# phi_q@KV of two token tiles back to back, one sign per PSUM slot, and three more AB buffers in the space of the first layernorm

## The chip, the core and the metric

The kernel runs on one core of a Trainium2 chip. A core has five engines that run side by side and are ordered only by semaphores: TensorE (PE in the profile; its weight loads are PEld), VectorE (DVE), ScalarE (ACT), GpSimd (POOL) and SyncE (SP), whose queue issues the DMAs here. Matmuls write to PSUM, eight banks of 512 fp32 columns on 128 partitions; the other engines copy results from there to SBUF. The metric is the device time of one execution in microseconds (us): the median of the runs.

## The reference

One block of a transformer on x of 2048 tokens by 640 columns: layernorm, linear attention with 32 heads of 20 columns and a Hedgehog feature map, output projection, residual; then layernorm, a gated GELU feed-forward of width 1536, residual.

```python
pq = einsum("bhsd,hdf->bhsf", q, w_phi);  pk = einsum("bhsd,hdf->bhsf", k, w_phi)
phi_q = concatenate([softmax(pq), softmax(-pq)], -1)     # 20 + 20 features a head
phi_k = concatenate([softmax(pk), softmax(-pk)], -1)
kv  = einsum("bhsf,bhsd->bhfd", phi_k, v);  z = einsum("bhsf->bhf", phi_k)
num = einsum("bhqf,bhfd->bhqd", phi_q, kv)
den = einsum("bhqf,bhf->bhq", phi_q, z)[..., None] + 1e-6
h   = x + (num / den).reshape(B, S, D) @ wo
h2  = h + (gelu(ln(h) @ w_gate) * (ln(h) @ w_up)) @ w_down
```

## The kernel before

The tokens are 16 tiles of 128, in four blocks of four (b = t // 4). Everything is written in the order in which it is to be issued, engine by engine; semaphores come from a tile framework that tracks who writes and who reads each buffer.

*First part, to about 90 us.* Layernorm of x, transposed into LN1T (one tile of 5 x 512 bf16 columns a block), then v, k, their features, and the sums over tokens (kv). The q features are computed with the tokens along the free dimension: `q_mm` multiplies the folded weights Wq2 with LN1T into `pq`, and `q_exp` writes exp(pq) and exp(-pq) into the 13 tiles Eq. The last `pq` matmuls are the last readers of LN1T.

*Attention of a tile, in stages.* `attn_a_mm` (L500) computes `ab`: for each sign s (the two softmaxes) and each of 5 groups of heads, two matmuls of 64 rows by 88 columns, one for each half u of the partitions, which lie next to each other in TensorE's 128 rows. The 20 matmuls of a tile write two PSUM slots: half u of the heads in slot u, the sign in the slot's bank. `attn_a_ev` (L515) copies both to the SBUF tile AB of fp32, of which there are two. `attn_b` (L526), `attn_b2` and `attn_b3` turn AB into the normalised attention output `o`: products and sums on POOL (`pr`, `den`, `w`), the reciprocal `rd` and the big product `tt` on VectorE. A DMA transpose (`attn_t`) gives oT; `attn_c` multiplies with Wo into `po`; `attn_d` (L574) adds the residual on VectorE; `attn_d2` finds the second layernorm's statistics on ACT and POOL; `attn_e` normalises on ACT and transposes by DMA into LN2T.

*Feed-forward.* `gate_up(b, f, a0, a1)` (L610) computes one of 12 chunks of 128 hidden columns: ten matmuls into one slot `gu`, gate in bank 0 and up in bank 1; GELU on ACT; the product GT on VectorE. `down(b, tl, u)` (L623) computes one tile's output in two halves of 320 columns, u = 0 and 1, in the two banks of one slot `pd`, 12 matmuls each; after u = 1 a single VectorE add of 640 columns takes both banks and the residual to y, which is stored three units later. Only the very last tile evicts its halves apart, and there the second half takes a slot of its own (L627).

*PSUM.* After the first part the pool `psG2` (L490) has four slots of two banks, shared by pq, ab, po, gu and pd. A slot is handed on when its last reader is done; the first matmul of its next user waits for that.

*The order around the change.* `weave` (L657) walks through a list of units (12 `gate_up`, then `down`s), and before unit i issues every attention stage whose index is at most i. Stages whose index lies past the end of a list are carried to the next. `attn_at(t, i, offs)` places tile t's stages at i plus an offset each. Tiles 0 to 2 get their `ab` before the first unit; tile 3 at unit 1, tiles 4, 5, 6 at units 6, 9, 13 of the first list and 7 at the start of the second; tiles 8 to 15 at units 0, 2, 5, 7 of blocks 1 and 2. So each `ab` block but the first three stands alone between units of the feed-forward. TensorE, VectorE, ACT, POOL and SP each run their own instructions in this order.

Of the kernel before, what the change touches and what calls it, by code (L numbers as in the profile page):

```python
# [8 lines left out]
BF16 = mybir.dt.bfloat16  # L9
F32 = mybir.dt.float32  # L10
ALU = mybir.AluOpType
# [6 lines left out]
def kernel(  # L18
# [12 lines left out]
    nc = tc.nc  # L31
    P = 128
    S = 2048
    D = 640
    H = 32
# [3 lines left out]
    NB = NT // 4  # L39
    NC = D // P  # L40
    NF = FF // P
# [17 lines left out]
    KC = Dh + 2  # L59


    UH = H // 2
# [3 lines left out]
    o_v = out.rearrange("b (p t) d -> p (b t) d", t=NT)  # L66
# [10 lines left out]
    x_sb = [const.tile([P, 4, D], BF16, name=f"x_sb{b}") for b in range(NB)]  # L77
# [14 lines left out]
    def eq(t, c, s):  # L92
        for E, g in zip(Eq, QG):
            if t // 4 * NC + c in g:
                return E[:, g.index(t // 4 * NC + c), s, t % 4 * P:(t % 4 + 1) * P]

    def small(pool, shape, name, bufs=3):
        return pool.tile(shape, F32, name=name, bufs=bufs)

    def gtile(name):  # L100
        return psG.tile([P, 2, 512], F32, name=name, tag="G")
# [40 lines left out]
    def transpose_to(dst, src, on_pe, on_dve=False):  # L142

        if on_pe:
            tp = psG.tile([P, 16, P], BF16, name="tp", tag="G")
            for c in range(NC):
                nc.tensor.transpose(tp[:, c, :], src[:, c * P:(c + 1) * P], ident)
            (nc.vector.tensor_copy if on_dve else nc.scalar.copy)(dst, tp[:, 0:NC, :])  # L148
        else:
            nc.sync.dma_start_transpose(dst, src)  # L150


    mid = ctx.enter_context(tc.tile_pool(name="mid", bufs=1, side="right"))
    LN1T = [mid.tile([P, NC, 512], BF16, name=f"LN1T{b}") for b in range(NB)]
    Wq2 = mid.tile([P, NC, D], BF16, name="Wq2")
    p1_cm = tc.tile_pool(name="p1", bufs=1, reuse_waits="tile")
    p1 = p1_cm.__enter__()
# [99 lines left out]
    def ln_ap(t, on_act=False, on_pe=False):  # L257
# [3 lines left out]
        else:  # L261
            transpose_to(LN1T[t // 4][:, :, t % 4 * P:(t % 4 + 1) * P], ln, False)

    def ln_tp(t, on_dve=False):
        transpose_to(LN1T[t // 4][:, :, t % 4 * P:(t % 4 + 1) * P], lnp[t], True, on_dve)

    def lnT(t, c):
        b, tl = divmod(t, 4)
        return LN1T[b][:, c, tl * P:(tl + 1) * P]

# [85 lines left out]
    def q_mm(j):  # L356

        pqs[j] = gtile("pq")
        for i, bc in enumerate(QG[j]):
            b, c = divmod(bc, NC)  # L360
            for kc in range(NC):
                nc.tensor.matmul(pqs[j][:, i, :], lhsT=Wq2[:, kc, c * P:(c + 1) * P], rhs=LN1T[b][:, kc, :],  # L362
                                 start=(kc == 0), stop=(kc == NC - 1))

    def q_exp(j, signs=(0, 1)):
        for s in signs:
            nc.scalar.activation(Eq[j][:, :, s, :], pqs[j][:, 0:len(QG[j])], ACTF.Exp, scale=(1.0, -1.0)[s])  # L367
# [23 lines left out]
    def tr_c(t):  # L391
        transpose_to(LN1T[0][:, :, t * P:(t + 1) * P], xc[t], True, t == 1)

# [100 lines left out]
    p2r = ctx.enter_context(tc.tile_pool(name="p2r", bufs=1, side="right", reuse_waits="tile"))  # L494
    Wd = p2r.tile([P, NF, D], BF16, name="Wd")
    nc.sync.dma_start(Wd, B_w_down.rearrange("(c p) n -> p c n", p=P))

    LN2T, st = {}, {}

    def attn_a_mm(t):  # L500

        b = t // 4
        if b not in LN2T:
            LN2T[b] = p2.tile([P, NC, 512], BF16, name="LN2T", bufs=2)
        AB = p2r.tile([P, 2, H, KC], F32, name="AB", bufs=2)
        ab = gtile("ab"), gtile("ab")
        for s in range(2):
            for c in range(NC):
                for u, r in enumerate(HALF):
                    nc.tensor.matmul(ab[u][:, s, 3 * c * KC:(3 * c + 4) * KC], lhsT=eq(t, c, s)[r],  # L510
                                     rhs=KV[r, c, s].rearrange("p h f -> p (h f)"),
                                     start=(c == 0), stop=(c == NC - 1), skip_group_check=True)
        st[t] = AB, ab

    def attn_a_ev(t, dve=0):  # L515
        AB, ab = st[t]
        for u in range(2):
            (nc.vector.tensor_copy if u >= 2 - dve else nc.scalar.copy)(  # L518
                AB[:, :, u * UH:(u + 1) * UH].rearrange("p s h f -> p s (h f)"), ab[u][:, :, 0:UH * KC])
        st[t] = AB  # L520

    def attn_a(t, dve=0):
        attn_a_mm(t)
        attn_a_ev(t, dve)

    def attn_b(t, on_pe=False):  # L526

        eng = nc.vector if on_pe else nc.gpsimd
        AB = st[t]
        pr = small(p2, [P, H, 2], "pr", 2)  # L530
        eng.tensor_tensor(pr, AB[:, 0, :, Dh:KC], AB[:, 1, :, 0:KC:KC - 1], ALU.mult)
        den = small(p2, [P, H], "den", 2)
# [71 lines left out]
    def attn_e(t, on_pe=False, on_dve=False):  # L604
        if not on_pe:
            attn_ln(t)
        ln = st[t]
        transpose_to(LN2T[t // 4][:, :, t % 4 * P:(t % 4 + 1) * P], ln, on_pe, on_dve)
# [14 lines left out]
    def down(b, tl, u):  # L623
        if u == 0:
            st["pd"] = gtile("pd"), p2.tile([P, D], BF16, name="y", bufs=4)
        pd, y = st["pd"]
        if u == 1 and b == NB - 1 and tl == 3:  # L627
            pd = gtile("pd")
        last = b == NB - 1 and tl == 3

        cuts = [(0, 192), (192, HD)] if last and u == 1 else [(0, HD)]
        for n0, n1 in cuts:
            if n0:
                pd = gtile("pd")
            for f in range(NF):
                nc.tensor.matmul(pd[:, u, n0:n1], lhsT=st[b, "g", f][:, tl * P:(tl + 1) * P],  # L636
                                 rhs=Wd[:, f, u * HD + n0:u * HD + n1], start=(f == 0), stop=(f == NF - 1))
            if u == 1 or last:
                a = u if last else 0
                r = lambda x: x.rearrange("p (u f) -> p u f", u=2)[:, a:u + 1, n0:n1]  # L640
                nc.vector.tensor_tensor(r(y), pd[:, a:u + 1, n0:n1], r(x_sb[b][:, tl, :]), ALU.add)  # L641
                f0, f1 = a * HD + n0, u * HD + n1
                stores.append((lag, o_v[:, 4 * b + tl, f0:f1], y[:, f0:f1]))
                if b == NB - 1 and tl >= 2:
                    store(lag)

    later, stores, lag = [], [], 3

    def store(n):

        stores[:] = [(i - n, *x) for i, *x in stores]
        while stores and stores[0][0] <= 0:
            _, dst, src = stores.pop(0)
            nc.sync.dma_start(dst, src)


    def weave(units, stages):  # L657

        stages = sorted(later + stages, key=lambda x: x[0])
        later.clear()  # L660
        for i, (fn, *args) in enumerate(units):
            while stages and stages[0][0] <= i:
                _, g, *a = stages.pop(0)
                g(*a)
            store(1)
            fn(*args)
        later.extend((i - len(units), g, *a) for i, g, *a in stages)

    def gus(b, a0, a1):
        return [(gate_up, b, f, a0, a1) for f in range(NF)]  # L670

    def downs(b, tls):
        return [(down, b, tl, u) for tl in tls for u in range(2)]


    q_mm(q)
    attn_a(0, 1)
    q_exp(q)
    q_mm(q + 1)
    attn_b(0, True)  # L680
    attn_b2(0, True)
    attn_b3(0, True)
    attn_a(1, 1)
    q_exp(q + 1)
    q_mm(q + 2)
    attn_t(0)
# [21 lines left out]
        q_exp(j)  # L708
    attn_ln(1, True)
    attn_e(1, True, True)  # L710
    attn_a(2, 2)
    assert q + 9 == len(Eq)

    def attn_at(t, i, offs):

        fns = (attn_a, attn_b, attn_b2, attn_b3, attn_c, attn_d, attn_d2, attn_e)
        return [(i + o, fn, t) for fn, o in zip(fns, offs) if o >= 0]

    SHORT = (0, 2, 3, 4, 9, 9, 10, 12)
    SHORT2 = (0, 2, 3, 4, 10, 10, 11, 13)  # L720
    LONG = (0, 1, 2, 3, 6, 6, 7, 8)


    weave(gus(0, 0, 256) + downs(0, (0, 1)),
          attn_at(2, 0, (-1, 0, 1, 2, 7, 7, 8, 10)) + attn_at(3, 1, SHORT) + attn_at(4, 6, SHORT2) + attn_at(5, 9, SHORT2) +
          attn_at(6, 13, SHORT2))
    weave(gus(0, 256, 512) + downs(0, (2, 3)), attn_at(7, 0, SHORT))
    for b in range(1, NB):
        stages = []
        if b + 1 < NB:  # L730
            for tl in range(4):
                stages += attn_at(4 * b + 4 + tl, (0, 2, 5, 7)[tl], LONG)
        weave(gus(b, 0, 512) + downs(b, range(4)), stages)
    man_cm.__exit__(None, None, None)


# [28 lines left out]
```

## Time and profile before

| | |
|---|---|
| Time, median of 3 runs | 280.23 us (279.33 to 280.53) |
| Span of the profiled execution | 277.2 us; its own time is not listed apart from the runs |
| Granted TensorE clock | 1.000 |
| Busy share: PE, DVE, ACT, POOL | 98%, 60%, 52%, 34% |
| TensorE, `gu` matmuls 512 columns wide, all | 89.5 us busy |
| TensorE, `pd` matmuls, all | 53.8 us busy |
| TensorE, `ab` matmuls x320 | 9.1 us busy, 204 ns each |
| ACT copies AB<-ab, 704 columns | 28, 748 ns each |
| VectorE copies AB<-ab, 704 columns | 4, 886 ns each |
| VectorE adds y<-pd, 640 columns | 15, 823 ns each |

The span runs from the first to the last instruction of one execution; the time is measured around the whole program and is longer. In the groups, a row is: line, engine, operation, output<-inputs, shapes, count | busy time in all, mean ns of one | idle time of the engine just before them and what ended it. Busy time of matmuls counts overlapping ones once: they are pipelined, so the distance from one start to the next is shorter than one's length. In the timeline a row is start, length, engine, line, operation; what stands in brackets is the engine's idle time before it and the instruction that ended that. The chain is the work that ended last, followed back through whatever released each piece.

### The profile page before, as it was taken

To read this page: it belongs to the slowest core of one execution; us is meant where nothing else is said; L and a number is where in the kernel's file an instruction comes from. 1 tells how busy PE (TensorE), PEld (TensorE's weight loads), DVE (VectorE), ACT (ScalarE), POOL (GpSimd) and SP (SyncE) were. 2 spreads that over 40 slices of the span, in tenths; PEclk is the share of its full clock that TensorE was granted. 3 is DMA by queue.
4 is the path that set the end of the run, shared out by engine and by line. 5 is a ranking of instruction groups with operands and counts; after the bars stand their busy time and mean duration, and the time that the engine had idled before them with its cause. 6 is when DMAs were issued, how large, how long until landed. Compare 5 with 4: busy or idle time off the path is not lost.

```text
span 277.2 us, 5817 instructions
## 1 busy us (share of the span) xinstructions
PE 271.6 (98%) x2337; PEld 172.1 (62%) x2337; DVE 167.3 (60%) x292; ACT 143.5 (52%) x239; POOL 94.7 (34%) x213
## 2 busy tenths in 40 slices
PE   7899999999999999999999999999999999999995
PEld 3677777764555887788754555675455567444574
DVE  6799999899496776675325757322666622233222
ACT  4879998778598755374524364413445440222200
POOL 4348997765202217365301353400226230000000
PEclk9999999999999999999999999999999999999999
DMA  7965732489730021324120213130022413000011
GB/s 204 192 232 112 99 74 47 44 256 393 255 102 0 4 47 36 85 49 77 30 65 2 47 27 63 32 88 33 14 36 25 73 25 95 26 0 0 0 50 47
DMA packets 42235, 21.37 MB, mean 77 GB/s; under 512 B 35040, under 2 KB 40416, under 8 KB 42208
## 3 DMA queue, kind: packets, MB, share of 16 engines
q1 hardware_dynamic: 42208, 21.01, 30.8%
q8 instruction: 18, 0.29, 0.5%
q14 instruction: 9, 0.07, 0.1%
HBM read 10.18 MB, written 2.62 MB: 46 GB/s over the span
## 4 chain that ended last, share of the span: by engine, by line
PE 87%; SPq 3%; DMA 3%; DVE 2%; ACT 2%; issue 1%
PE gu L615 38%; PE pd L636 19%; PE pq L362 8%; PE po L570 8%; PE pk L274 5%; PE pv L274 4%; PE ab L510 3%; PE kvp L340 2%; SPq L186 2%; DMA LN1T<-ln 2%; DVE stats L110 1%; DMA WkT<-in_A_wqkv_dram 1%; ACT E L307 1%; ACT ln L134 1%; PE wa L228 1%
## 5 line engine op out<-in xcount | busy, mean ns | idle before, releaser
L621 DVE TENSOR_TENSOR GT<-gu,g 128x512 bf16<-128x512 f32 (+1 forms) x60 | 34.4, 580 | 54.3 <-ACT g L618 54.1
L618 ACT ACTIVATE g<-gu 128x512 bf16<-128x512 f32 (+1 forms) x60 | 30.7, 512 | 69.3 <-PE gu L615 68.5
L615 PE MATMUL gu<-LN2T,Wg 128*128 128x512 bf16 (+1 forms) x300 | 61.9, 337 | 0.1
L615 PE MATMUL gu<-LN2T,Wu 128*128 128x512 bf16 (+1 forms) x300 | 61.8, 337 | 0.0
L636 PE MATMUL pd<-Wd,GT 128*128 128x320 bf16 (+2 forms) x396 | 53.8, 295 | 0.0
L636 PEld LDWEIGHTS <-GT 128*128 128x128 bf16 x396 | 37.9, 98 | 15.3 <-DVE GT L621 0.9
L615 PEld LDWEIGHTS <-Wu 128*128 128x128 bf16 x300 | 29.3, 98 | 22.6
L615 PEld LDWEIGHTS <-Wg 128*128 128x128 bf16 x300 | 28.3, 98 | 20.8
L274 PEld LDWEIGHTS <-LN1T 128*128 128x128 bf16 x290 | 27.9, 98 | 11.0 <-DMA LN1T<-ln 0.3
L322 POOL TENSOR_TENSOR vt<-vS,rs 128x672 bf16<-128x672 bf16 x22 | 29.1, 1344 | 9.1 <-DVE rs L318 7.4
L641 DVE TENSOR_TENSOR y<-pd,x_sb 128x640 bf16<-128x640 f32 (+3 forms) x18 | 13.5, 749 | 30.2 <-PE pd L636 30.2
L518 ACT COPY AB<-ab 128x704 f32<-128x704 f32 x28 | 19.6, 748 | 19.8 <-PE ab L510 19.6
L551 DVE TENSOR_TENSOR tt<-AB,w 128x1280 bf16<-128x1280 f32 x16 | 23.8, 1486 | 1.0 <-POOL w L544 0.9
L570 PE MATMUL po<-Wo,oT 128*128 128x320 bf16 x160 | 24.3, 299 | 0.0
L274 PE MATMUL pk<-Wk,LN1T 128*128 128x320 bf16 x160 | 24.0, 299 | 0.0
L314 DVE TENSOR_REDUCE sk<-E 128x64 f32<-128x1280 bf16 x16 | 22.9, 1434 | 1.2 <-ACT E L307 1.2
L362 PE MATMUL pq<-LN1T,Wq 128*128 128x512 bf16 x100 | 22.9, 379 | 0.0
L367 ACT ACTIVATE Eq<-pq 128x1024 bf16<-128x1024 f32 (+1 forms) x26 | 19.9, 830 | 2.4 <-PE pq L362 2.4
L307 ACT ACTIVATE E<-pk 128x640 bf16<-128x640 f32 x28 | 18.3, 716 | 4.5 <-PE pk L274 4.3
L570 PEld LDWEIGHTS <-oT 128*128 128x128 bf16 x160 | 15.6, 98 | 7.0 <-ACT oT L148 0.3
L274 PE MATMUL pv<-Wv,LN1T 128*128 128x320 bf16 x130 | 19.8, 299 | 0.2 <-DMA LN1T<-ln 0.2
L134 ACT ACTIVATE ln<-x_sb,v,rstd 128x640 bf16<-128x640 bf16 x14 | 12.9, 919 | 11.3 <-POOL v L598 11.1
(101 smaller groups left out, 268.1 us busy)
## 6 DMA issues: line engine op xcount, KB each, us to landing
out_dram<-y SPq DMA_DIRECT2D x15, 160.0 KB, 1.8
Wg<-in_B_w_gate_dram SPq DMA_DIRECT2D x1, 1920.0 KB, 9.4
Wu<-in_B_w_up_dram SPq DMA_DIRECT2D x1, 1920.0 KB, 15.3
Wd<-in_B_w_down_dram SPq DMA_DIRECT2D x1, 1920.0 KB, 7.9
x_sb<-in_A_x_dram SPq DMA_DIRECT2D x2, 640.0 KB, 5.5
Wo<-in_A_wo_dram SPq DMA_DIRECT2D x1, 800.0 KB, 11.1
x_sb<-in_A_x_dram SPq DMA_DIRECT2D x4, 160.0 KB, 3.1
Wv<-in_A_wqkv_dram SPq DMA_DIRECT2D x2, 320.0 KB, 4.1
```

The lines of the kernel that those rows point to most:

```text
L274: nc.tensor.matmul(ps[:, u, 0:HD], lhsT=lnT(t, c), rhs=W[:, c, u * HD:(u + 1) * HD], start=(c == 0), stop=(c == NC - 1))
L307: nc.scalar.activation(Ek[t][:, s, :].rearrange("p (u f) -> p u f", u=2), pk[:, :, 0:HD], ACTF.Exp, scale=((lnp[t][2], nrstd[t]) if t in C ...
L314: nc.vector.reduce_sum(sk, Ek[t].rearrange("p s (h f) -> p (s h) f", f=Dh), axis=AX.X)
L322: eng.tensor_tensor(vt[:, s], vS[t % 8], rs[:, s * H:(s + 1) * H, None].to_broadcast([P, H, VC]), ALU.mult)
L362: nc.tensor.matmul(pqs[j][:, i, :], lhsT=Wq2[:, kc, c * P:(c + 1) * P], rhs=LN1T[b][:, kc, :], start=(kc == 0), stop=(kc == NC - 1))
L367: nc.scalar.activation(Eq[j][:, :, s, :], pqs[j][:, 0:len(QG[j])], ACTF.Exp, scale=(1.0, -1.0)[s])
L551: nc.vector.tensor_tensor(tt.rearrange("p s (h f) -> p s h f", f=Dh), num, w[:, :, :, None].to_broadcast([P, 2, H, Dh]), ALU.mult)
L570: nc.tensor.matmul(po[:, u, 0:HD], lhsT=st[t][:, c, :], rhs=Wo[:, c, u * HD:(u + 1) * HD], start=(c == 0), stop=(c == NC - 1))
L615: nc.tensor.matmul(gu[:, i, 0:n], lhsT=W[:, c, f * P:(f + 1) * P], rhs=LN2T[b][:, c, a0:a1], start=(c == 0), stop=(c == NC - 1))
L618: nc.scalar.activation(g[:, 0:n], gu[:, 0, 0:n], ACTF.Gelu_apprx_tanh)
L621: nc.vector.tensor_tensor(st[b, "g", f][:, a0:a1], gu[:, 1, 0:n], g[:, 0:n], ALU.mult)
L636: nc.tensor.matmul(pd[:, u, n0:n1], lhsT=st[b, "g", f][:, tl * P:(tl + 1) * P], rhs=Wd[:, f, u * HD + n0:u * HD + n1], start=(f == 0), sto ...
```

## The change

Four edits go together.

1. *One sign per slot.* A slot of `ab` now holds both halves u of one sign s (`ab[s][:, u]`), so the first slot is complete after 10 of the 20 matmuls. `attn_a_ev` copies one sign, or one half of it, on the engine it is given.
2. *Pairs.* `attn_pair(t)` issues the 40 matmuls of tiles t and t + 1 in a row, in all four slots, and then five copies: the first slot half on ACT and half on VectorE, the second on ACT, the third on VectorE, the fourth on ACT. Tiles 2 to 15 go in seven pairs; 0 and 1 stay single, one slot on ACT and one on VectorE.
3. *Five AB buffers.* The four LN1T tiles become views of one fp32 tile, and three more AB buffers are views of the same memory.
4. *Places.* The pairs stand before unit 0 (tiles 2, 3), at units 7 and 14 of the first list, 14 and 16 of the second, and 18 and 20 of block 1; an index equal to the list's length means the start of the next list. All later stages keep the unit they had. In the five `down` tiles listed in AHEAD, the halves are 384 and 256 columns and each is added to y by itself; a pair follows right after each of these five tiles.

```diff
-    LN1T = [mid.tile([P, NC, 512], BF16, name=f"LN1T{b}") for b in range(NB)]
+    LN1F = mid.tile([P, NB * NC * 256], F32, name="LN1T")
+    LN1T = [LN1F.bitcast(BF16).rearrange("p (b c n) -> p b c n", b=NB, c=NC)[:, b] for b in range(NB)]
...
+    ABs = [p2r.tile([P, 2, H, KC], F32, name=f"AB{i}") for i in range(2)]
+    ABs += [LN1F[:, i * 2 * H * KC:(i + 1) * 2 * H * KC].rearrange("p (s h f) -> p s h f", s=2, h=H) for i in range(3)]
...
-        AB = p2r.tile([P, 2, H, KC], F32, name="AB", bufs=2)
+        AB = ABs[t % len(ABs)]
...
-                    nc.tensor.matmul(ab[u][:, s, 3 * c * KC:(3 * c + 4) * KC], lhsT=eq(t, c, s)[r],
+                    nc.tensor.matmul(ab[s][:, u, 3 * c * KC:(3 * c + 4) * KC], lhsT=eq(t, c, s)[r],
...
-    def attn_a_ev(t, dve=0):
+    def attn_a_ev(t, s, eng, us=(0, 2)):
         AB, ab = st[t]
...
+        eng(AB[:, s].rearrange("p (u h) f -> p u (h f)", u=2)[:, us[0]:us[1]], ab[s][:, us[0]:us[1], 0:UH * KC])
+
+    def attn_a(t):
         attn_a_mm(t)
-        attn_a_ev(t, dve)
+        attn_a_ev(t, 0, nc.scalar.copy)
+        attn_a_ev(t, 1, nc.vector.tensor_copy)
+        st[t] = st[t][0]
+
+    def attn_pair(t):
+        attn_a_mm(t)
+        attn_a_mm(t + 1)
+        attn_a_ev(t, 0, nc.scalar.copy, (0, 1))
+        attn_a_ev(t, 0, nc.vector.tensor_copy, (1, 2))
+        attn_a_ev(t, 1, nc.scalar.copy)
+        attn_a_ev(t + 1, 0, nc.vector.tensor_copy)
+        attn_a_ev(t + 1, 1, nc.scalar.copy)
+        for i in (t, t + 1):
+            st[i] = st[i][0]
...
+        if (b, tl) in AHEAD:
+            f0, f1 = ((0, 384), (384, D))[u]
+            for f in range(NF):
+                nc.tensor.matmul(pd[:, u, 0:f1 - f0], lhsT=st[b, "g", f][:, tl * P:(tl + 1) * P],
+                                 rhs=Wd[:, f, f0:f1], start=(f == 0), stop=(f == NF - 1))
+            nc.vector.tensor_tensor(y[:, f0:f1], pd[:, u, 0:f1 - f0], x_sb[b][:, tl, f0:f1], ALU.add)
+            if u == 1:
+                stores.append((lag, o_v[:, 4 * b + tl, :], y))
+            return
...
-    attn_a(2, 2)
+    attn_pair(2)
...
+    EARLY = (0, 1, 2, 7, 7, 8, 10)
+    SHORT = (0, 1, 2, 8, 8, 9, 11)
+    LONG = (0, 1, 2, 5, 5, 6, 7)
+    AHEAD = {(0, 0), (0, 2), (0, 3), (1, 2), (1, 3)}
...
+          attn_at(2, 0, EARLY) + attn_at(3, 3, EARLY) + [(7, attn_pair, 4)] + attn_at(4, 8, SHORT) + attn_at(5, 11, SHORT) +
+          [(14, attn_pair, 6)] + attn_at(6, 15, SHORT) + attn_at(7, 18, EARLY))
+    weave(gus(0, 256, 512) + downs(0, (2, 3)),
+          [(14, attn_pair, 8), (16, attn_pair, 10)] + attn_at(8, 17, LONG) + attn_at(9, 19, LONG) + attn_at(10, 22, LONG) +
+          attn_at(11, 24, LONG))
+    weave(gus(1, 0, 512) + downs(1, range(4)),
+          [(18, attn_pair, 12), (20, attn_pair, 14)] + attn_at(12, 21, LONG) + attn_at(13, 23, LONG) +
+          attn_at(14, 26, LONG) + attn_at(15, 28, LONG))
+    for b in (2, 3):
+        weave(gus(b, 0, 512) + downs(b, range(4)), [])
```

More of the change, by code (lines that the diff above doesn't have):

```diff
@@ L513, in attn_a_mm @@
         st[t] = AB, ab
-    def attn_a_ev(t, dve=0):
+    def attn_a_ev(t, s, eng, us=(0, 2)):
         AB, ab = st[t]
[L517 to L522, printed above, removed]
-        attn_a_mm(t)
-        attn_a_ev(t, dve)
+        eng(AB[:, s].rearrange("p (u h) f -> p u (h f)", u=2)[:, us[0]:us[1]], ab[s][:, us[0]:us[1], 0:UH * KC])
+    def attn_a(t):
+        attn_a_mm(t)
+        attn_a_ev(t, 0, nc.scalar.copy)
[11 more added lines that the diff above has]
+            st[i] = st[i][0]
     def attn_b(t, on_pe=False):
@@ L676 @@
     q_mm(q)
-    attn_a(0, 1)
+    attn_a(0)
     q_exp(q)
@@ L682 @@
     attn_b3(0, True)
-    attn_a(1, 1)
+    attn_a(1)
     q_exp(q + 1)
@@ L710 @@
     attn_e(1, True, True)
-    attn_a(2, 2)
+    attn_pair(2)
     assert q + 9 == len(Eq)
     def attn_at(t, i, offs):
[L716 to L721, printed above, removed]
-    weave(gus(0, 0, 256) + downs(0, (0, 1)),
[L725 to L733, printed above, removed]
+        return [(i + o, fn, t) for fn, o in zip((attn_b, attn_b2, attn_b3, attn_c, attn_d, attn_d2, attn_e), offs)]
+    EARLY = (0, 1, 2, 7, 7, 8, 10)
+    SHORT = (0, 1, 2, 8, 8, 9, 11)
+    LONG = (0, 1, 2, 5, 5, 6, 7)
+    AHEAD = {(0, 0), (0, 2), (0, 3), (1, 2), (1, 3)}
+    weave(gus(0, 0, 256) + downs(0, (0, 1)),
+          attn_at(2, 0, EARLY) + attn_at(3, 3, EARLY) + [(7, attn_pair, 4)] + attn_at(4, 8, SHORT) + attn_at(5, 11, SHORT) +
[8 more added lines that the diff above has]
+        weave(gus(b, 0, 512) + downs(b, range(4)), [])
     man_cm.__exit__(None, None, None)
```

## The prediction

> **What bounds the kernel now.** I read the engine shares and the clock on the page first, then the chain that ended last, then the timeline around one block of the edited matmuls, then the groups by form.
>
> ```profile
> PE 271.6 (98%) x2337; PEld 172.1 (62%) x2337; DVE 167.3 (60%) x292; ACT 143.5 (52%) x239; POOL 94.7 (34%) x213
> ...
> PEclk9999999999999999999999999999999999999999
> ...
> PE 87%; SPq 3%; DMA 3%; DVE 2%; ACT 2%; issue 1%
> ```
>
> TensorE is busy for the whole span at full clock, and the chain runs on it. From 92 us on that chain holds nothing but TensorE pieces, end to end, until the last eviction. So any time that TensorE loses or gains after 90 us is the kernel's time, and other engines count only where TensorE waits for them.
>
> Timeline around the `ab` block of tile 4 (start, length, engine, line):
>
> ```profile
> 97.48 0.71 PE L615 MATMUL gu<-LN2T,Wu 128*128 128x256 bf16 x5
> ...
> 98.12 0.57 PE L510 MATMUL ab<-KV,Eq 64*128 64x88 bf16 x20
> ...
> 98.62 0.72 PE L615 MATMUL gu<-LN2T,Wg 128*128 128x256 bf16 x5
> ```
>
> The 256-column matmuls start 0.109 us apart (ten take 1.09 in the chain), so the five from 97.48 are issued out at 98.03. The first `ab` starts 0.10 later. Its twenty go in ten pairs 0.039 apart (0.39 in all); then 0.11 is lost again before `gu` at 98.62. A block costs 0.60, of which 0.20 is getting in and out.
>
> Groups by form, timeline at the KV mask, at the second layernorm's first transposes, and on VectorE before the first `down`:
>
> ```profile
> L641 DVE TENSOR_TENSOR y<-pd,x_sb 128x640 bf16<-128x640 f32 x15 | 12.3, 823 | 28.6 <-PE pd L636 28.6
> ...
> L518 DVE COPY AB<-ab 128x704 f32<-128x704 f32 x4 | 3.5, 886 | 1.5 <-PE ab L510 1.5
> ...
> L641 DVE TENSOR_TENSOR y<-pd,x_sb 128x320 bf16<-128x320 f32 x1 | 0.5, 491 | 0.8 <-PE pd L636 0.8
> ```
> ```profile
> 71.20 0.51 ACT L349 COPY acc<-kvp 128x420 f32<-128x420 f32 x1 [0.82 <-DVE kvp L348]
> 71.74 0.59 DVE L352 TENSOR_TENSOR KV<-kvp,kmask 128x420 bf16<-128x420 f32 x1 [0.57 <-ACT acc L349]
> ```
> ```profile
> 90.34 0.49 DVE L148 COPY LN2T<-tp 128x640 bf16<-128x640 bf16 x1 [0.72 <-PE tp L147]
> ...
> 90.88 0.71 PE L615 MATMUL gu<-LN2T,Wg 128*128 128x256 bf16 x5
> 91.16 1.28 ACT L618 ACT_TABLE_LOAD   x1
> ```
> ```profile
> 111.41 0.35 DVE L540 RECIPROCAL rd<-den 128x32 f32<-128x32 f32 x1 [1.46 <-POOL den L533]
> ```
>
> The KV pair matters most: ACT reads one bank of the PSUM tile kvp, VectorE reads the other, they share no data, and VectorE still waited 0.57 for ACT. Waits here are kept per PSUM tile, not per bank. Handoffs: VectorE to TensorE 0.05 (90.83 to 90.88); TensorE to VectorE, TensorE to ACT and ACT to VectorE 0.03 to 0.04 (the last 128-column `pd` ended at 274.30 and its add began at 274.34).
>
> **The change, part by part.**
>
> *Joining blocks.* Seven pairs each drop one entry and one exit: 7 x 0.20 = -1.4 us. For pair 2 it is inside that pair's count below, so -1.2 for the other six. No offset in the stages behind an `ab` block moves: `attn_b` to `attn_e` of each tile keep their unit, only the `ab` matmuls and copies come sooner.
>
> *The 384/256 split in five `down`s.* The columns are the same: 12 x 0.163 + 12 x 0.109 against 24 x 0.136. But both halves lie in one PSUM tile `pd`, and the first is evicted before the second is written. In the changed program's order with its waits, the first 256-column matmul waits for exactly the 384-wide add; before, the second half of these tiles had no such wait, since one add took both halves at the end. So TensorE stands still for: the last 384 matmul's own length of about 0.33 (0.30 at 320 columns, 0.38 at 512), 0.04, the add, 0.05, less the 0.16 that a step costs anyhow. The add: 290, 359, 491 and 823 ns at 128, 192, 320 and 640 columns lie on a line, 557 at 384. Hold: 0.33 + 0.04 + 0.56 + 0.05 - 0.16 = 0.81 (0.80 before rounding), if VectorE is free.
>
> It is free at four of the five. In the first (block 0, tile 0) the reciprocal of tile 5 stands ahead of the add in VectorE's queue, and that waits for POOL. In the trace it started at 111.41, 2.74 after the `down` began at 108.67 in the chain, and its chain (tile 3's statistics, then `pr`, `den`) does not move. The add then starts 2.74 + 0.27 (the next operation begins about 0.08 before an end) = 3.0 after the `down`'s start, ends at 3.57, and the second half starts at 3.62 where 1.96 was due: hold 1.66. Sum 4 x 0.80 + 1.66 = **+4.9**. Bounds: 4.0 (nothing ahead of the add), 6.4 (a 1.49 `tt` ahead of it once more). A gain is excluded: the add needs the twelfth matmul.
>
> *Slots.* A pair needs all four PSUM slots, so the next unit needs the first `ab` slot back. Its eviction is split, half on ACT, half on VectorE; in the changed program's waits VectorE's half stands behind ACT's in every pair, as at 71.74. From the first `ab` matmul: sign 0 done at 0.36 (0.16 + 0.20 length), ACT half 0.40 to 0.85 (746 ns at 704 columns; the two GELU forms, 385 and 597 ns at 256 and 512, give 0.84 ns a column, so 0.45 at 352), VectorE half 0.88 to 1.40 (886 less 352 x 1.04), TensorE at 1.45. The pair's own matmuls would let it go on at 0.88: hold 0.57. The 256 add (0.43) behind the last slot is back just in time. Pairs 8, 10, 12, 14: 4 x 0.57 = **+2.3**.
> Pair 4 follows `po` of tile 2, whose residual add (0.82) frees the fourth slot: 0.39 there, then VectorE's half after it, 0.26: **+0.65**. Pair 6 follows the first `down`: VectorE has `tt` 1.49 and `o` 0.49 of tile 5 between the two adds, so the fourth slot is 0.33 late and the first 0.17: **+0.5**.
> Bounds for the slots: 0.09 each if the halves ran side by side, so 0.5 in all; 0.9 each, 5.4, if VectorE were behind by another 0.3.
>
> *Pair 2, at the start.* Its first ACT half stands behind the last two exponentials (to 91.14): half to 91.6, VectorE's to 92.1, `gu` 0 at 92.15 instead of 90.88, while tile 3's block (0.60) is gone from after it: **+0.67**. The 1.28 table load used to run at 91.16 under `gu` 0; now it stands behind three copies, at about 92.7, so GELU 0 starts at about 94.0 against 92.45. The slots stand that (`gu` 4 needs it at 96.5). The tile 2 attention behind it does not: reciprocal, `tt` at 95.7 against 94.78, `o` done at 97.7, and its DMA transpose takes 2.6 from issue: landed at 100.3, where `po` would start at 99.8: **+0.5** (from 0, if GELU keeps its place, to 1.0).
>
> *Nothing:* the three new AB buffers lie in LN1T's space, whose readers, the `pq` matmuls, are issued ahead; the first 90 us keep their order and waits. ACT loses about seven of its copies and VectorE gains them, with 40% idle. If that cover went, each copy would cost at most its 0.89.
>
> Sum: 4.9 + 2.3 + 0.65 + 0.5 + 0.67 + 0.5 - 1.2 = **+8.2 us**. The profiled execution's span is 277.2; its own time is not listed, but the three runs, 279.33 to 280.53, put 2.1 to 3.3 around it. On the median 280.23 this gives **288.4**.
>
> The Trainium skill speaks against the largest term: "PSUM — Partial Sum Buffer", section on bank collisions, says that engines collide only on the same bank and quadrant and that different banks run clean. By that alone TensorE could write the second half, in another bank, during the add; the term would be 0 and the sum +3.3. The 0.57 at 71.74 is a wait between two banks of one tile, so I go by the row: the chip may allow the overlap, the program's semaphores do not.
>
> **Rivals.**
> *Banks go their own way (other side).* If TensorE passes the second half and the slots without being held, the joins are left: -1.4, 278.8. It decides once the hold per split `down` is under 1.4 / 5 = 0.29. Against it: the add alone is 0.56, and 71.74. For it: VectorE is 40% idle.
> *The halves run side by side.* Only the splits hold: 4.9 + 4 x 0.09 + 0.3 + 0.4 + 0.3 + 0.5 - 1.2 = +5.6, 285.8. For it: ACT and VectorE copied tile 0's `ab` at the same time (73.76 and 73.82), but from two tiles.
> *Held attention.* VectorE's lateness also reaches four more transposes of `oT` or LN2T, 0.5 each as in tile 2: +10.2, 290.4. Against it: TensorE is as late as they are.
>
> **How the numbers follow.** Forecast 0.70, side by side 0.14, held attention 0.10, banks free 0.04, something unnamed 0.02. The forecast alone spans 286.8 to 289.9 (slots and splits off by their handoffs, tile 2's wait from 0 to 1.0). With the neighbours on both sides: 284.8 to 290.5. A change under 0.5%, 1.4 us, can't be told from none here. Faster 0.04, same 0.02, slower 0.94.
>
> **What would show it.** The waits view must show TensorE waiting for VectorE's y five times, about 0.8 each and once about 1.7, and for VectorE's AB copy about seven times, about 0.5; the chain should pass through both. The by-form groups should show the 384 add near 0.56. Joined blocks should take 0.99 from entry to exit. TensorE's busy share falls to about 95%. I am wrong if the second half starts before the first add ends, or if ACT's and VectorE's halves of one slot overlap.

## The result, and the profile after

The changed kernel takes 287.74 us (median of five runs, 287.60 to 288.30), the kernel before 279.37 in the same session. The ratio is 1.0296 (95% interval 1.0273 to 1.0319): 8.4 us slower, where the forecast had 8.2.

The profiled execution took 288.3 us, of which 286.6 are the span: 9.4 more than the 277.2 before. Of these, 0.4 came before 90 us, in work that the change hardly touches: TensorE's last transposes of the second layernorm start at 90.25 instead of 89.86. From there to the start of the last `down`s TensorE takes 180.09 us against 171.11. That distance, 8.98 longer, holds all of the change, and I use it below for every run ("the stretch"). It is steadier than the time: over the ten traces of this case these transposes started anywhere from 89.62 to 90.73.

Engine shares, granted clock and shares of the chain on the page of the changed kernel:

```profile
PE 272.2 (95%) x2324; PEld 173.4 (61%) x2337; DVE 175.3 (61%) x309; ACT 138.7 (48%) x234; POOL 94.0 (33%) x213
...
PEclk9999999999999999999999999999999999999999
...
PE 82%; DVE 5%; SPq 3%; issue 3%; ACT 2%; POOL 2%; DMA 1%; POOLq 0%
```

TensorE is as busy in microseconds as before (272.2 against 271.6) and its clock is full; the span has grown around it. VectorE has risen from 2% of the chain to 5%, and POOL, which was not named on it, has 2%.

What TensorE waits for, from the view of waits (engine and line, what released it: us in total, times, longest):

```profile
PE pd L649 <- DVE y L651: 4.5, 5, 1.9
...
PE gu L629 <- DVE LN1T L520: 1.0, 2, 0.5
PE pd L649 <- DVE LN1T L520: 1.0, 2, 0.5
PE po L584 <- DMA oT<-o: 0.7, 1, 0.7
PE gu L629 <- DVE AB L520: 0.5, 1, 0.5
...
PE ab L513 <- DVE y L651: 0.4, 1, 0.4
```

The first row is the five split `down`s. The rows with LN1T and AB are copies out of `ab` slots (LN1T is the memory under three of the AB buffers). These idle times are a little shorter than the holds, because a matmul is shown for its whole length though the next is due before its end. I measure a hold as the distance from one matmul's start to the next, less the usual distance.

One split `down` and the pair behind it, in the chain (start, length, piece), and the pair in the timeline:

```profile
139.65 1.96 PE pd L649 x12
141.61 0.02 issue
141.63 0.57 DVE y L651
142.20 0.04 issue
142.25 1.47 PE pd L649 x12
143.71 0.32 PE ab L513 x10
144.04 0.02 issue
144.06 0.46 ACT LN1T L520
144.52 0.02 issue
144.54 0.53 DVE LN1T L520
145.08 0.04 issue
145.12 2.12 PE pd L649 x12
```
```profile
143.65 0.96 PE L513 MATMUL ab<-KV,Eq 64*128 64x88 bf16 x40
```

TensorE stops twice. At 141.6 the second half of the `down` waits for the add of the first. Then it starts `ab`, at 143.65 (the chain counts that piece only from the end of the matmul before it, 143.71), and the chain leaves it after ten matmuls, the first slot; ACT copies one half, then VectorE the other, one behind the other, and only then the next `down` begins, at 145.12. From the first `ab` at 143.65 to there are 1.47 us, 1.57 with the entry; two single blocks cost 1.20 before, entries included.

The groups by form of VectorE, columns as before:

```profile
L651 DVE TENSOR_TENSOR y<-pd,x_sb 128x384 bf16<-128x384 f32 x5 | 2.7, 545 | 5.0 <-PE pd L649 5.0
L520 DVE COPY LN1T<-ab 128x352 f32<-128x352 f32 x5 | 2.6, 525 | 1.8 <-ACT LN1T L520 1.8
L651 DVE TENSOR_TENSOR y<-pd,x_sb 128x256 bf16<-128x256 f32 x5 | 2.1, 423 | 6.2 <-PE pd L649 6.2
```

The 384 add takes 545 ns (557 forecast), the 256 add 423 (0.43), the half copy 525 (0.52), and that copy's idle time is put down to ACT. ACT's half copies take 454 and 452 (0.45).

### The profile page after: what moved, and what is told of

Same layout as the page of the kernel before. It is cut to its first block, busy times and chain, and to the rows that moved or that the text cites. A ratio compares the mean times of both kernels' runs of the same rounds, so it can differ in the third digit from the quotient of the medians.

```text
span 286.6 us, 5822 instructions
## 1 busy us (share of the span) xinstructions
PE 272.2 (95%) x2324; PEld 173.4 (61%) x2337; DVE 175.3 (61%) x309; ACT 138.7 (48%) x234; POOL 94.0 (33%) x213
## 4 chain that ended last, share of the span: by engine, by line
PE 82%; DVE 5%; SPq 3%; issue 3%; ACT 2%; POOL 2%; DMA 1%; POOLq 0%
PE gu L629 32%; PE pd L659 13%; PE pk L275 8%; PE pq L363 7%; PE po L584 7%; PE pv L275 6%; PE pd L649 5%; PE kvp L341 2%; SPq L187 2%; DVE tt L565 2%; DMA WkT<-in_A_wqkv_dram 1%; DVE y L651 1%; ACT LN1T L520 1%; PE ab L513 1%; DVE LN1T L520 1%
## 5 line engine op out<-in xcount | busy, mean ns | idle before, releaser
L629 PE MATMUL gu<-LN2T,Wg 128*128 128x512 bf16 (+1 forms) x291 | 61.2, 335 | 2.2 <-DVE LN1T L520 1.0
L629 PEld LDWEIGHTS <-Wg 128*128 128x128 bf16 x300 | 29.3, 98 | 23.1 <-issue 1.5
L659 PE MATMUL pd<-Wd,GT 128*128 128x320 bf16 (+2 forms) x276 | 37.2, 293 | 0.1
L664 DVE TENSOR_TENSOR y<-pd,x_sb 128x640 bf16<-128x640 f32 (+3 forms) x13 | 9.4, 722 | 22.6 <-PE pd L659 22.6
L649 PE MATMUL pd<-Wd,GT 128*128 128x384 bf16 (+1 forms) x120 | 17.9, 299 | 5.5 <-DVE y L651 4.5
```

Of the source, the lines that this page charges most:

```text
L629: nc.tensor.matmul(gu[:, i, 0:n], lhsT=W[:, c, f * P:(f + 1) * P], rhs=LN2T[b][:, c, a0:a1], start=(c == 0), stop=(c == NC - 1))
L649: nc.tensor.matmul(pd[:, u, 0:f1 - f0], lhsT=st[b, "g", f][:, tl * P:(tl + 1) * P], rhs=Wd[:, f, f0:f1], start=(f == 0), stop=(f == NF - 1))
```

## The experiments

Eight kernels were run. E1 to E4, E7 and E8 are edits of the changed kernel; E5 adds one part to the kernel before; E6 keeps the new buffers and slots and takes the rest back. "Before" was 279.03 beside E1, E2, E3 and E5, and 279.38 beside E4, E6, E7 and E8.

### E1: no split

```diff
-    AHEAD = {(0, 0), (0, 2), (0, 3), (1, 2), (1, 3)}
+    AHEAD = ()
```

> The changed kernel with the set AHEAD empty: every down writes 320 + 320 columns and is evicted by one add of 640. Theory (waits are kept per PSUM tile): the four holds of 0.81 and the one of 2.0 at the 384-column add are gone, -5.3. In pairs 8 to 14 the later 640 add (0.82) delays the fourth slot by 0.4, but the first slot's copy chain is the later one anyway, so their hold stays at 0.57. In pair 6 the 640 add now stands behind rd, tt (1.49) and o (0.49) of tile 5, so the fourth slot comes about 2.6 late: +2.6. Net -2.7: about 285.0. Rival (the splits cost nothing, the time is lost elsewhere): 287.7 or more, since the larger add frees the slot later.

Measured: 285.15, ratio 1.0235 (1.0197 to 1.0272); the stretch is 6.10 longer than before, not 8.98. Without the split the five holds are gone, and part of them returns elsewhere. The chain at pair 6, and the pair's last ten `ab` in the timeline:

```profile
113.99 0.36 DVE rd L554
...
114.94 1.50 DVE tt L565
116.44 0.02 issue
116.46 0.49 DVE o L569
116.95 0.73 DVE y L664
117.69 0.44 DVE AB L520
118.13 0.04 issue
118.17 3.42 PE pd L659 x24
```
```profile
117.74 0.37 PE L513 MATMUL ab<-KV,Eq 64*128 64x88 bf16 x10 [2.52 <-DVE y L664]
```

The whole add of 640 columns now stands behind rd, tt and o of tile 5 in VectorE's queue, and the pair's fourth slot is the one it frees: TensorE stands still for 2.70 before the last ten `ab` (0.55 in the changed kernel). In pairs 8 to 14 the fourth slot comes 0.40 late, and what is left of the first slot's wait is 0.32 at the exit, of which 0.13 is the usual exit: together 0.58 a pair, the same as with the split. So the split costs 5.27 and saves 2.15, all of that at pair 6: 8.98 - 5.27 + 2.15 gives 5.86. The other 0.24 of the 6.10 lies in the first `down`, which takes 3.61 from its start to the first `ab`, where E2 has 3.36 for the same columns: two of its matmuls wait for VectorE's last GT.

### E2: a slot of its own for the second half

```diff
             f0, f1 = ((0, 384), (384, D))[u]
+            if u == 1:
+                pd = gtile("pd")
```

> The split stays, but the second half, 256 columns, goes to a PSUM slot of its own. Theory: no wait between the halves is left, so the four holds of 0.81 vanish, -3.25; at tile (0, 0) the hold of 2.0 vanishes, but the 256 add still stands behind rd, tt and o of tile 5, so pair 6 waits for its fourth slot about 2 instead: -0.5 there. About 284.0. If the hold came from the chip (a matmul kept out of PSUM while VectorE reads it) and not from the tile's bookkeeping, it would stay in part: 286 to 287.7.

Measured: 285.16 (284.28 to 287.09), ratio 1.0207 (1.0186 to 1.0228). Two of the five executions, the profiled one (287.09) and one of 286.02, had a mean granted clock of 0.994; the other three took 284.28 to 285.16. The same `down` as in the chain above, in the timeline of TensorE and then of VectorE:

```profile
141.50 3.42 PE L651 MATMUL pd<-Wd,GT 128*128 128x384 bf16 x24
144.85 0.96 PE L513 MATMUL ab<-KV,Eq 64*128 64x88 bf16 x40
```
```profile
143.65 0.56 DVE L653 TENSOR_TENSOR y<-pd,x_sb 128x384 bf16<-128x384 f32 x1 [1.05 <-PE pd L651]
```

All 24 matmuls run through, 3.35 from the first to the first `ab`, while the add reads the other slot from 143.65 to 144.21. All five holds are gone, with the same columns, the same adds and the same engines. What held TensorE was the order that the program asked for, one PSUM tile with a reader still in it, and not the chip: it writes one bank while VectorE reads another without delay. (Two banks of the same slot at once were not tried.) This is also what the Trainium skill says in "PSUM — Partial Sum Buffer", in the section on bank collisions; the prediction was right to go by the row, since the rule speaks of what the chip allows and not of what the program waits for.

Pair 6 paid part of it back again, mostly at its fourth slot (`PE ab L513 <- DVE y L653`, 2.2 idle), for the reason seen in E1: it took 3.43 from its first matmul to the next unit and 1.57 in the changed kernel, so 1.87 more. The stretch is 7.28 longer than before, but this execution also lost clock. Busy time by stretch, granted clock in the column before the DMA share:

```profile
118.00:123.00 5.00, 5.00 (x30) 3.08 (x26) 0.89 (x2) 0.74 (x1) 0.60 (x2) 0.66 0.26 66
123.00:124.40 1.40, 1.40 (x12) 1.02 (x11) 0.82 (x1) 0.00 (x0) 0.00 (x0) 1.00 0.04 12
```

The `down` of 24 matmuls there took 4.94 from start to start instead of 3.26. Less these 1.68 the stretch is 5.60 longer, which agrees with 8.98 - 5.27 + 1.87 = 5.58.

### E3: the reciprocal of tile 5 behind the first add

```diff
-          ... + attn_at(5, 11, SHORT) +
+          ... + attn_at(5, 11, (0, 4, 4, 8, 8, 9, 11)) +
```

> Only the offsets of tile 5: its reciprocal, w, tt and o are issued three units later, after pair 6, so that nothing of POOL's chain stands ahead of the 384 add of tile (0, 0). Theory: that hold falls from 2.0 to 0.81, and pair 6 falls from 0.67 to 0.57: -1.3, about 286.4. Rival (the long hold at this place is something else, such as the first use of the down weights): no change, 287.7.

Measured: 287.08, ratio 1.0287 (1.0267 to 1.0308). The chain at the first `down`:

```profile
110.89 1.96 PE pd L649 x12
112.86 0.02 issue
112.88 0.57 DVE y L651
113.45 0.04 issue
113.49 1.47 PE pd L649 x12
114.97 0.32 PE ab L513 x10
```

It now looks like the four others: the add starts the moment the twelfth matmul is through, and the hold is 0.81 instead of 2.03. The stretch shrinks by 1.30 against the changed kernel, and the profiled time by 1.34 (286.96 against 288.30). The median fell by only 0.7 in another session, against a before that was 0.3 faster there; where the first part happens to end accounts for as much. The excess of the first hold, 1.22, is thus the reciprocal's place in VectorE's queue.

### E4: the first slot copied whole by ACT

```diff
-        attn_a_ev(t, 0, nc.scalar.copy, (0, 1))
-        attn_a_ev(t, 0, nc.vector.tensor_copy, (1, 2))
-        attn_a_ev(t, 1, nc.scalar.copy)
-        attn_a_ev(t + 1, 0, nc.vector.tensor_copy)
-        attn_a_ev(t + 1, 1, nc.scalar.copy)
+        attn_a_ev(t, 0, nc.scalar.copy)
+        attn_a_ev(t, 1, nc.vector.tensor_copy)
+        attn_a_ev(t + 1, 0, nc.scalar.copy)
+        attn_a_ev(t + 1, 1, nc.vector.tensor_copy)
```

> In each pair the first slot is copied whole by ACT and the second whole by VectorE, the third by ACT, the fourth by VectorE; nothing else. Theory (the first slot comes back only after two half copies in a row): back at 0.40 + 0.75 + 0.05 = 1.19 after the first ab matmul in place of 1.45, so the hold falls from 0.57 to 0.31 in pairs 8 to 14, and by about as much at pairs 2 and 6; pair 4's falls more, since VectorE's half behind the residual add is gone. -1.6: about 286.1. Rival (the halves run side by side, the hold has another cause): the first slot comes back later than before with 0.75 in one piece, +0.2 each: 289.

Measured: 286.47, ratio 1.0261 (1.0237 to 1.0285); the stretch is 7.25 longer than before, 1.73 less than with the change. The same pair in the timeline:

```profile
143.42 0.96 PE L513 MATMUL ab<-KV,Eq 64*128 64x88 bf16 x40
...
143.83 1.39 ACT L520 COPY LN1T<-ab 128x704 f32<-128x704 f32 x2 [2.19 <-PE ab L513]
...
144.03 1.69 DVE L520 COPY LN1T<-ab 128x704 f32<-128x704 f32 x2
...
144.63 1.78 PE L648 MATMUL pd<-Wd,GT 128*128 128x384 bf16 x10 [0.25 <-ACT LN1T L520]
```

TensorE goes on 1.21 after the first `ab`, not 1.47, and its releaser is ACT. ACT's and VectorE's copies overlap here, since each has a slot of its own: an engine that reads a whole slot in 0.76 gives it back sooner than two that read half each in turn (0.45 and 0.52, and the handoff). The hold at the exit falls from 0.58 to 0.32 in four pairs (1.07 together); pair 2 wins 0.27, pair 4 0.18, pair 6 0.13, and `po` of tile 2 0.10.

### E5: the split alone, in the kernel before

```diff
+        if (b, tl) in AHEAD:
+            f0, f1 = ((0, 384), (384, D))[u]
+            for f in range(NF):
+                nc.tensor.matmul(pd[:, u, 0:f1 - f0], lhsT=st[b, "g", f][:, tl * P:(tl + 1) * P],
+                                 rhs=Wd[:, f, f0:f1], start=(f == 0), stop=(f == NF - 1))
+            nc.vector.tensor_tensor(y[:, f0:f1], pd[:, u, 0:f1 - f0], x_sb[b][:, tl, f0:f1], ALU.add)
+            ...
+    AHEAD = {(0, 0), (0, 2), (0, 3), (1, 2), (1, 3)}
```

> The kernel before with nothing but the 384/256 split in the same five tiles; no pairs, no other AB buffers. Theory: four holds of 0.81; at tile (0, 0) the ab block of tile 6 (0.6) stands between the halves and covers part of a hold of about 1.7, so 1.1. Sum +4.3: about 283.7. Rival (the pairs are the whole cost): 279.4, as before.

Measured: 283.65, ratio 1.0170 (1.0151 to 1.0189); the stretch is 4.76 longer. Two of the waits view's lines for TensorE are new:

```profile
PE pd L635 <- DVE y L637: 3.7, 5, 1.1
...
PE po L570 <- DMA oT<-o: 0.2, 1, 0.2
```

Four holds of 0.81, as in the changed kernel. The fifth, in block 0's first tile, is 1.18 here and not 2.03, because the single `ab` block of tile 6 stands between the two halves and covers some of it. Another 0.35 is a `po` in block 2, the second line, that now waits for its transposed oT. More than half of the whole loss (4.76 of 8.98) thus comes without a single joined block.

### E6: everything apart again

The changed kernel's five AB buffers and one sign per slot, but every tile's `ab` at the unit it had before, and no split:

```diff
-    attn_pair(2)
+    attn_a_mm(2)
+    attn_a_ev(2, 0, nc.vector.tensor_copy)
+    attn_a_ev(2, 1, nc.vector.tensor_copy)
+    ...
-          ... + [(7, attn_pair, 4)] + ... + [(14, attn_pair, 6)] + ...
+          ... + [(1, attn_aa, 3)] + [(6, attn_aa, 4), (9, attn_aa, 5)] + ... + [(13, attn_aa, 6), (16, attn_aa, 7)] + ...
```

Tiles 8 to 15 go the same way, one at a time; `attn_aa` is the block of one tile with both copies on ACT.

> One sign per slot, five AB buffers in LN1T's space and the same offsets of the later stages, but every tile's ab block alone at the unit that it had in the kernel before, one slot copied by ACT and... for tiles 3 to 15 both by ACT, tile 2 both by VectorE; no split. Theory: these parts cost nothing, so the time is that of the kernel before, 279.4 within 0.5%. Rival (the shared space of LN1T or the new slot layout costs): 281 or more.

Measured: 279.01, ratio 0.9996 (0.9980 to 1.0011), the stretch 0.02 longer. Its waits view names TensorE only in the first part of the kernel, as before. The buffers and the sign per slot cost nothing and bring nothing; all of the change's price lies in the joins and the split.

### E7: tiles 2 and 3 apart

```diff
-    attn_pair(2)
+    attn_a_mm(2)
+    attn_a_ev(2, 0, nc.vector.tensor_copy)
+    attn_a_ev(2, 1, nc.vector.tensor_copy)
+    st[2] = st[2][0]
...
-          attn_at(2, 0, EARLY) + attn_at(3, 3, EARLY) + ...
+          attn_at(2, 0, EARLY) + [(1, attn_aa, 3)] + attn_at(3, 3, EARLY) + ...
```

> The changed kernel, but tiles 2 and 3 stand apart as in the kernel before: tile 2 ahead of the first unit with both copies on VectorE, tile 3 at unit 1 with both on ACT. Theory: the table load of GELU is again hidden under the first unit, the first slot of pair 2 is not waited for (-0.6), and the po of tile 2 no longer waits for the DMA of its oT (-0.87 in the trace): -1.5, about 286.2. Rival (the start of the weave costs nothing): 287.7.

Measured: 286.92, ratio 1.0281 (1.0257 to 1.0306); the stretch is 7.80 longer, 1.18 less than with the change. `po` of tile 2 in the changed kernel, then in this one, each with what stands ahead of it:

```profile
99.59 0.71 PE L629 MATMUL gu<-LN2T,Wu 128*128 128x256 bf16 x5
...
101.00 1.53 PE L584 MATMUL po<-Wo,oT 128*128 128x320 bf16 x10 [0.70 <-DMA oT<-o]
```
```profile
99.15 0.71 PE L635 MATMUL gu<-LN2T,Wu 128*128 128x256 bf16 x5
100.01 1.53 PE L590 MATMUL po<-Wo,oT 128*128 128x320 bf16 x10
```

With the usual 0.54 for five `gu` matmuls, `po` is 0.87 late in the first and 0.31 in the second. Pair 2's 0.62 is gone, and 0.56 of the wait for oT; 0.31 of it stays although VectorE and ACT begin as before. I had expected all of it to go. What is missing is TensorE's own work: before, the `ab` block of tile 4 (0.60) ran at 98.12, between the units ahead of that `po`, and covered the transpose. Joined with tile 5, it runs after the `po`. In E6, where this block stands at its old place again, no `po` waits.

### E8: all the holds that had an edit, off together

The edits of E2, E3, E4 and E7 in one kernel. Six of the seven pairs stay, at their units.

> Six pairs, with all holds that were named taken away or shortened: the second half in its own slot, tile 5's stages after pair 6, the first slot whole on ACT, tiles 2 and 3 apart. Theory: what is left against the kernel before is six joins of -0.20 and six first-slot holds of 0.31, and 0.3 at pair 4: +0.9, about 280.3. Rival (some of the loss is not in the named holds): 282 or more. If the joins are worth what they promise and the holds are gone altogether: 278.5.

Measured: 280.06, ratio 1.0035 (1.0019 to 1.0052); the stretch is 0.97 longer. TensorE's waits after the first part are few and short:

```profile
PE pd L656 <- ACT LN1T L520: 0.5, 2, 0.3
...
PE pd L666 <- ACT AB L520: 0.2, 1, 0.2
PE gu L634 <- ACT AB L520: 0.2, 1, 0.2
PE gu L634 <- ACT LN1T L520: 0.2, 1, 0.2
PE ab L513 <- DVE x_sb L603: 0.2, 1, 0.2
```

Five pairs still wait 0.32 for ACT's copy of the first slot, pair 4 waits 0.41 for its fourth slot behind the residual add of tile 2, and `po` of tile 2 is 0.31 late: 2.3 against the 1.2 that six joins save, so 1.1 on balance where 0.97 was measured. That is less than the 0.5% which I count as a change, but the interval leaves no room for a gain: even so, the joins do not pay for the waits that they bring.

## Why the prediction was right, step by step

All holds are TensorE's in the trace of the changed kernel, in us.

| Step | predicted | measured |
|---|---|---|
| Split, four tiles, each | 0.80 | 0.81, 0.81, 0.81, 0.81 |
| Split, block 0 tile 0 | 1.66 | 2.03 |
| First slot, pairs 8, 10, 12, 14, each | 0.57 | 0.58 |
| Pair 4: fourth slot, first slot | 0.39 + 0.26 | 0.41 + 0.18 |
| Pair 6: fourth slot, first slot | 0.33 + 0.17 | 0.55 + 0.13 |
| Pair 2 | 0.67 | 0.62 |
| `po` of tile 2 | 0.5 | 0.87 |
| Joins, six | -1.2 | -1.2 |
| Sum | +8.2 | +9.2 |

*The split.* The mechanism is the one in the prediction: the second half waits for exactly the 384 add (chain at 141.63), and E2 shows that it is the shared PSUM tile that makes it wait. E5 gives the same 0.81 without any pair. The term that was mis-sized is the first tile: the add stood behind the reciprocal as said, but that started 3.16 after the `down`, not 2.74 (the hold grew by 0.37 only, since this one add took 0.49 and not 0.56). Of the 0.42, 0.17 is mine: I took the `down`'s start from the chain (108.67), where the timeline of before has 108.50. The other 0.25 is a link that did move: tile 3's residual add, which starts POOL's statistics, began 1.82 after its `po` (107.21 to 109.03) and before only 1.56 (104.96 to 106.52). The prediction said that this chain "does not move".

*The slots.* VectorE's half stood behind ACT's in every pair, as at the KV mask. E4 takes this order away and with it the part of the hold that it makes. The half copies took 454 and 525 ns, as worked out; ACT's 0.84 ns a column should have been 0.83 (212 ns over 256 columns), which changes neither. In pair 6 the prediction let `tt` of tile 5 follow the 384 add at once. In the trace it waited 0.18 for POOL's `w` (from 114.67 to 114.86), and by about that much the pair was held longer than forecast, 0.68 against 0.50.

*Pair 2 and the oT of tile 2.* The place and the chain were right: the table load now runs at 93.20, behind the copies, and moves GELU, the reciprocal and `tt` of tile 2. `po` was held 0.37 more than taken. The term that was mis-sized is `o`: with the 0.39 of the start taken off, `tt` began at 95.80 (95.7 forecast) but took 1.63, not the 1.48 it had in the trace of before, so `o` was done at 97.96 instead of 97.7. Why this one `tt` was slower, no run here shows. `po` itself was due 0.06 sooner than I had it. The transpose took its 2.6. The forecast had counted that tile 4's block no longer stands ahead of this `po`; my expectation of E7 forgot it.

*Put at nothing.* The new buffers cost nothing, as E6 shows. ACT lost eight and a half copies and not about seven (28 were 704 columns wide before; now 16 are, and 7 half as wide). No run tests that by itself, but no wait of TensorE after 90 us is left over for it: the waits view puts them all down to the terms of the table.

*Why the median is nearer than the sum.* The prediction's own terms add to 8.3 and not to the 8.2 that stands there. Measured they add to 9.2, so they missed by 0.9, and the stretch grew by 8.98 (the other 0.2 is spread over distances that differ by hundredths). The median is only 8.4 above the one of before in its session, since the profiled execution was the slowest of the five (288.3 against 287.6 to 288.0) and that of before near the fastest of its five (278.91): in every execution listed the time is 1.7 to 1.8 longer than the span, so a span of 277.2 goes with 278.9 and not with the 279.33 to 280.53 that the prediction put around it. And the base of the forecast, 280.23, lay 0.9 above the before of that session. Part of the agreement to 0.7 us is therefore luck.

*The rivals.* "Banks go their own way" fell to the first waits row, and E2 shows that the chip would have allowed what that rival needs, once the halves lie in two slots. "The halves run side by side" fell to the chain at 144.06 and 144.54. "Held attention" fell to a single wait on an oT transfer in the whole stretch, that of tile 2. TensorE's busy share is the 95% that was forecast. For VectorE's copy of the first slot it waited about 0.5 five times and not seven: in pairs 4 and 6 the fourth slot made most of the hold. What I wrote to look for in joined blocks, 0.99 from entry to exit, is not in the trace: it left out the hold that I had myself put there, and with it they take 1.57.

## What to carry to other kernels

Work out what a change asks of the buffers' bookkeeping and not only of the engines: two halves that are evicted apart want two PSUM slots, or the second one's matmuls wait for the first one's eviction, 0.81 us each time here. Joining blocks so that they fill every slot saves an entry and an exit (0.20 here) and puts an eviction of 0.3 to 0.6 on the path of the unit behind them; whether it pays with a slot left over, no run here shows. And before moving small blocks of matmuls, look whether they cover something where they stand, a DMA or an engine's queue: in E7 0.31 of a wait stayed because the block that had covered it runs later, and in E1 a wait grew from 0.55 to 2.70 because the add that frees the slot had moved behind other work of VectorE.

## What the runs showed that I had not expected

In E2's profiled execution the granted clock was 0.66 on average from 118 to 123 us, after TensorE had stood still for 2.2 us, and 24 matmuls took 1.68 longer: from 118.3 to 121.7, for 3.4 us, they started 0.267 apart and not 0.136. In E1's profiled execution the same place had a longer stop, 2.5 in the timeline, and no such loss behind it. But one of E1's other three executions, of 287.08 us against 284.78 and 284.79, had a mean clock of 0.994, as two of E2's five had; no execution of any other kernel listed was under 0.998. So the loss comes in some executions of one and the same kernel, and only in the two kernels with the longest stops. The Trainium skill, "TensorE: Matmul & The Clock Gate", part 1 on the clock gate, says that the clock is halved after at least one idle window of about 3.4 us, and that these windows run freely. One window at half clock would lose 1.7, an estimate from that page, and that is near the 1.68. But no stop here was as long as such a window: on that the page and the trace differ, and the trace decides. That the windows lie differently from one execution to the next would fit, but no run here shows it. A stop of TensorE may thus cost more than its own length.

The first part, whose work is nearly the same in all ten kernels, ended up to 1.1 us apart from one profiled execution to another (89.62 to 90.73), while the holds behind it agree to 0.02. A difference of half a microsecond between two medians of four or five runs says little here, and the distance between two landmarks on TensorE says more.
